# Attention and feed-forward on one core: softmax's two buffers alternate by batch, and side work of batches 3 to 7 is laid out over other steps

## The chip, the core and the metric

One core of a Trainium2 chip runs the whole program. TensorE (PE) multiplies matrices, VectorE (DVE) and ScalarE (ACT) work elementwise, GpSimd (POOL) hardly takes part, and SyncE (SP) issues the DMA transfers, all in one queue. Each engine works through its own instructions in order and waits at semaphores for the others. The metric is the device time of one execution in microseconds; lower is better.

## What is computed

```python
def attention(x, state):                 # B, H, S, D = 8, 8, 512, 64; state: 32 rows a head
    a = softmax(x @ state.T / sqrt(D));  xread = a @ state
    a2 = softmax(state @ x.T / sqrt(D)); sread = a2 @ x
    return concat([xread, sread])        # 544 rows for each of 8 batches, 512 columns

def ffn(x, w_in, w_out):                 # 4352 rows, 512 -> 2048 -> 512
    h = x @ w_in
    return (h - tanh(h)) @ w_out
```

All of it is float32. Matmuls run on operands that are split into a high and a low part (three products for one, lines 427 to 429 and 467 to 469); some small ones run on whole float32.

## The kernel before

**Chunks and steps.** The feed-forward part is the bulk. It runs in nine chunks: chunk `i` is batch `i`'s 512 rows of `xread` for `i` from 0 to 7, and chunk 8 is the 256 rows of `sread` of all batches. The 2048 hidden columns are taken in 16 pieces `f` of 128. One pair `(i, f)` is a step. `steps` lists them: 0 to 7 are the first half of chunk 0, 8 to 23 chunk 1, 24 to 31 the second half of chunk 0, and from 32 on chunks 2 to 8 with 16 steps each (batch 6 is steps 96 to 111). In a step `hidden` (six matmuls `hps`, lines 427 to 429) is written for the step two ahead (`LAG`), then `output` (twelve matmuls `ops`, lines 467 to 469) for the step itself. Between them `finish` makes `t = tanh(h)` on ACT, `t = h - t` on DVE (both line 435), and splits `t` into `g` (ACT line 119, DVE line 120). The bank that `hps` writes is one of two, so `hidden` of a step needs the subtraction of the step two before it.

**What attention leaves for it.** For chunk `i` the hidden piece is softmax times a product of state and input weights, `m`, which `load_m` brings in four loads a chunk (`mr`, line 241) and splits; for batches 6 and 7 a second addend `ml` is loaded and added on DVE (line 245). Softmax of batch `b` comes from `attention(b, aT)`, a generator whose pieces are: load `xT` and state (piece 0), scores `sps` on PE and softmax of each half (1 and 2), normalise, transpose and split into the tile `aT` for each half (3 and 4), then `state_read`.

**The state read.** `state_read` makes softmax over the other axis for each half (pieces 5 and 6). In each of them `regroup` transposes the half on DVE into `pe` (line 338), SP sends it to DRAM as `pd` (line 340) and loads it back in four transfers as `p2t` (line 343). Piece 7 is the read itself, 32 small matmuls `rps` (line 376), piece 8 scales it into `sr`. `pe` and softmax's tile `e` share two buffers. `xT` and `xn`, the input of the read, share two buffers too. Batches 0 and 1 do their softmax early and only their state reads late: `a0` and `late1` are such generators. At the end `turn_sread` regroups `sr` and splits it into `srT`, the input of chunk 8.

**Side work by a table.** The table `SCH` says at which step each piece of side work is written into the program: `att3` to `att7` hold the nine pieces of `attention` of batches 3 to 7, `a0` and `r1` the four of the late reads of batches 0 and 1, `m0` and `m1` the units that make `m`. `TURN` is the step of the first half of `turn_sread`. A step's side work may not be issued before that step's tanh and subtraction (`tc.issue_after`). Inside these bounds a scheduler sets the order on each engine from its own model, so that a piece can stand some steps away from its number.

**The two buffers.** `new_attention` takes one of two buffers for `aT`:

```python
aTs[b] = pool.tile([P, 2, 2, 512], F32R, tag="aT" if b % 4 in (1, 2) else "aT0", name=f"aT{b}", bufs=1)
```

So batches 3 and 4 follow each other in `aT0`, 5 and 6 in `aT`, batch 7 and then `srT` in `aT0`.

Of the kernel before, what the change touches and what calls it, by code (L numbers as in the profile page):

```python
# [9 lines left out]
F32R = mybir.dt.float32r  # L10
# [8 lines left out]
P = 128  # L19
# [12 lines left out]
LONE = 1  # L32
WHOLE_ROWS = 2
EARLY = 4
TURN = 123


@with_exitstack
def attention_ffn(ctx: ExitStack, tc: tile.TileContext, xT, xn, bd, bh, sp, sq, sm, sl, win, wout, xout, sout):
# [13 lines left out]
    pool = ctx.enter_context(tc.tile_pool(name="pool", bufs=2))  # L53
# [18 lines left out]
    wo = [cpool.tile([P, 2, DM], F32R, name=f"wo{f}") for f in range(NFF // 2)]  # L72
# [27 lines left out]
    pair = []  # L100
# [16 lines left out]
    def split(hi, lo, src, sub=None):  # L117

        nc.scalar.copy(hi, src)  # L119
        return (sub or nc.vector).tensor_sub(lo, src, hi)  # L120

    class Weight:
# [5 lines left out]
        def load(self):  # L128
            if self.src.dtype == F32:
                self.raw = next(raws)(f"{self.name}d", [P, 512], F32)  # L130
                dst = self.raw
            else:
                self.raw = next(raws)(f"{self.name}d", [P, 512, 2], U32)
                dst = self.raw.rearrange("p f w -> p (f w)")
            src = self.src.bitcast(dst.dtype)
            if len(src.shape) == 3:
                dst = dst.rearrange("p (r f) -> p r f", r=4)
            loadlog.append(nc.sync.dma_start(dst, src).ins)
# [19 lines left out]
                step()  # L158


    SCH = json.loads('{"conv": [8, 8, 9, 9, 11, 11, 12, 12], "pair": [10, 10, 13, 13], "a0": [57, 57, 59, 60], "att2": [12, 13, 13, 23, 27, 28, 29, 35, 39], "att3": [33, 38, 42, 43, 45, 46, 53, 55, 57], "att4": [54, 56, 60, 60, 60, 60, 60, 64, 67], "att5": [61, 69, 71, 71, 72, 72, 72, 74, 75], "att6": [87, 90, 90, 91, 93, 93, 94, 96, 98], "att7": [101, 101, 104, 104, 108, 108, 110, 112, 121], "m0": [19, 19, 19, 22, 22, 22, 22, 25, 25, 28, 28, 28, 30, 30, 30, 36], "m1": [50, 50, 53, 58, 61, 67, 67, 68, 77, 79, 79, 86], "wo": [8, 12, 12, 13, 13, 16, 19, 22], "r1": [75, 76, 79, 90], "at1": [8, 9], "at0": [10, 16], "plain": [1, 5, 6, 7]}')
    m_first = {}
    loadlog = []
    XH = int('5')
# [9 lines left out]
    def m_first_two(q, b):  # L174

        if b == 0:
            m = m_first[q] = pool.tile([P, 2, 512], F32, tag="mr", name=f"mr0{q}", bufs=RRB)
        else:
            m = m_second[q] = pool.tile([P, 2, 512], F32, tag=f"mr1{q}", name=f"mr1{q}", bufs=1)
        pss = [bank(ps_a, f"mps{b}{q}{k}") for k in range(2)]  # L180
        state_rows(pss, sps[:, 0, :, b], [wfs[q, r // 2][:, r % 2] for r in range(4)])
        for k in range(2):
            nc.scalar.copy(m[:, k], pss[k])
        if b == 0:
            nc.sync.dma_start(mdram[0][q][0].rearrange("g h n f -> (h n) g f"), m)
# [90 lines left out]
    def all_scores(b, bdr, xrs, pss=None):  # L276
        pss = pss or [bank(ps_a, f"sps{b}{hf}") for hf in range(2)]
        for j in reversed(range(4)):
            for hf in (0, 1) if b in SCH["plain"] else (1, 0):
                rs = slice(64 * hf, 64 * hf + 64)  # L280
# [53 lines left out]
    def regroup(src, name):  # L334


        e = pool.tile([P, 512], F32, tag="e", name=f"pe{name}")
        nc.vector.transpose(e, src)
        d = dram.tile([4, 32, 512], F32, name=f"pd{name}")
        nc.sync.dma_start(d.rearrange("j u x -> (j u) x"), e)  # L340
        dst = pool.tile([P, 4, 4, NS], F32, tag="p2t", name=f"p2t{name}", bufs=PTB)
        for c in range(4):
            nc.sync.dma_start(
                dst[32 * c : 32 * c + 32].rearrange("u j k n -> u j (k n)"),
                d[:, :, 128 * c : 128 * c + 128].rearrange("j u x -> u j x"),
            )
        return dst
# [42 lines left out]
    def turn_sread():  # L390
        turned = [regroup(sr[g].rearrange("p q k u -> p (q k u)"), f"t{g}") for g in range(2)]
        yield
        srT = pool.tile([P, 2, 4, 256], F32R, tag="aT0", name="srT", bufs=1)
        for g in range(2):
            hi, lo = (srT[:, i, :, P * g : P * g + P].rearrange("p k (b n) -> p k b n", b=4) for i in range(2))
            split(hi, lo, turned[g].rearrange("p b k n -> p k b n"))
        aTs[B] = srT
        yield
# [97 lines left out]
    aTs = [None] * (B + 1)  # L496
    ats = [[None] * 2 for _ in range(2)]

    def new_attention(b):
        aTs[b] = pool.tile([P, 2, 2, 512], F32R, tag="aT" if b % 4 in (1, 2) else "aT0", name=f"aT{b}", bufs=1)  # L500
        return attention(b, aTs[b])

    def advance(units, n=1):
        for _ in range(n):
            if next(units, 1) == 1:
                return
# [17 lines left out]
    def convert_win(q, p):  # L524
        if p % 2 == 0:
            wfs[q, p // 2] = pool.tile([P, 2, 512], F32, tag=("wf", "stage")[q - 2], name=f"w0{q}{p // 2}", bufs=WB)
        w0[q][p].convert(wfs[q, p // 2][:, p % 2])
        if p % 2:
            nc.sync.dma_start(wf[q][:, p - 1 : p + 1], wfs[q, p // 2])
# [317 lines left out]
    a0 = state_read(0, [ss[0], ss[1]])  # L847
# [3 lines left out]
    m1 = [m_units(g) for g in range(2)]  # L851
# [4 lines left out]
    wo_it = iter(range(HALF, NFF))  # L856

    turn = turn_sread()
    steps = [(0, f) for f in range(HALF)] + [(1, f) for f in range(NFF)] + [(0, f) for f in range(HALF, NFF)]
    steps += [(i, f) for i in range(2, B + 1) for f in range(NFF)]  # L860
    for st, (i, f) in list(enumerate(steps))[HALF:]:
        with ExitStack() as gates:
            for x in tanhs[st + (st < 2 * NFF)]:
                gates.enter_context(tc.issue_after(x))
            for _ in range(SCH["conv"].count(st)):
                convert_win(*next(convs))
                load(1)
            for _ in range(SCH["wo"].count(st)):
                x = next(wo_it)
# [12 lines left out]
        with ExitStack() as gates:  # L882
            for x in tanhs[st] if st < 2 * NFF else ():
                gates.enter_context(tc.issue_after(x))
            for _ in range(SCH["pair"].count(st)):
                m_first_two(*next(pairs))

        with ExitStack() as gates:
            if st < GATED:
                for x in tanhs[st]:  # L890
                    gates.enter_context(tc.issue_after(x))
            advance(a0, SCH["a0"].count(st))
            advance(second_split, SCH["at1"].count(st))
            advance(first_split, SCH["at0"].count(st))
            advance(late1, SCH["r1"].count(st))
            for b in range(2, B):
                n = SCH[f"att{b}"].count(st)
                if n:
                    if b not in atts:
                        atts[b] = new_attention(b)  # L900
                    advance(atts[b], n)
            for g in range(2):
                advance(m1[g], SCH[f"m{g}"].count(st))
            if st == TURN:
                advance(turn)
# [50 lines left out]
```

## Time and profile before

| what | value |
|---|---|
| median of 3 runs | 655.21 us (655.2 to 656.06) |
| the profiled execution | 655.09 us |
| its span, first to last instruction | 653.3 us |
| busy: PE, DVE, ACT | 640.9, 454.6, 347.1 us |
| granted TensorE clock, mean | 0.996 of full speed |
| DMA queue of SP | 104.56 MB, 49.9% of 16 engines |

The profile is of one execution. Busy time is the time in which an engine has an instruction in work; a matmul's printed duration overlaps with the next one, so that the pace of PE is read from the starts. "idle before" in brackets is how long the engine stood without work ahead of an instruction and whose event ended it.

### The profile page before, as it was taken

The page shows a single profiled execution, that of the slowest core. Times are in us where ns is not written, and L with a number is a line of the kernel's source. Part 1 is how long each engine was busy: PE and PEld are TensorE (multiplying, and loading weights), DVE is VectorE, ACT ScalarE, POOL GpSimd, SP SyncE. Part 2 cuts the span into 40 slices and gives each one's busy share as a digit, 9 for nine tenths or more (in the row PEclk, how much of TensorE's full clock was granted, in tenths as well). Part 3 has the DMA queues.
Part 4 walks back from the last instruction along what each step waited for, and adds up shares of the span by engine and source line. Part 5 has one row for each costly group of instructions (what it writes and reads, how often), then busy time and mean ns, then how long its engine had stood idle before and what let it go on. Part 6 is the DMA issues. An engine that isn't in the chain of part 4 may idle for free.

```text
span 653.3 us, 10246 instructions
## 1 busy us (share of the span) xinstructions
PE 640.9 (98%) x3818; PEld 504.6 (77%) x3818; DVE 454.6 (70%) x813; ACT 347.1 (53%) x629; POOL 0.7 (0%) x5
## 2 busy tenths in 40 slices
PE   8999999999999999999899999999799999999997
PEld 5456766888878788877677888887687888888996
DVE  5998999899584776566875985458756675464542
ACT  4864767777673545645455665444434443333442
POOL 0000000000000000000000000000000000000000
PEclk9999999999999999999999999999999999999999
DMA  8994786267786414446666248453542142021300
GB/s 317 379 312 149 255 282 262 55 194 221 241 281 188 131 57 137 130 137 193 198 204 174 92 153 277 129 161 133 173 150 97 33 129 97 1 77 53 130 32 33
DMA packets 65170, 105.34 MB, mean 161 GB/s; under 512 B 7648, under 2 KB 32224, under 8 KB 65120
## 3 DMA queue, kind: packets, MB, share of 16 engines
q1 hardware_dynamic: 64976, 104.56, 49.9%
q8 instruction: 30, 0.49, 0.3%
q14 instruction: 20, 0.16, 0.1%
q10 hardware_dynamic: 144, 0.13, 0.1%
HBM read 69.01 MB, written 35.65 MB: 160 GB/s over the span
## 4 chain that ended last, share of the span: by engine, by line
PE 86%; DVE 6%; DMA 5%; issue 1%; ACT 1%; SPq 0%; ACTq 0%; DVEq 0%
PE ops L467 17%; PE ops L469 17%; PE ops L468 17%; PE hps L427 9%; PE hps L429 8%; PE hps L428 8%; DMA pd<-pe 2%; PE hps L738 2%; PE mps L217 2%; PE rps L376 1%; PE mps L682 1%; PE ops L764 1%; PE mps L216 1%; DMA p2t<-pd 1%; DMA mearly<-e 1%
## 5 line engine op out<-in xcount | busy, mean ns | idle before, releaser
L467 PE MATMUL ops<-wo,g 128*128 128x512 f32 x536 | 213.7, 400 | 0.0
L468 PE MATMUL ops<-wo,g 128*128 128x512 f32 x536 | 209.0, 390 | 0.0
L469 PE MATMUL ops<-wo,g 128*128 128x512 f32 x536 | 196.2, 390 | 0.0
L435 DVE TENSOR_TENSOR t<-hps,t 128x512 f32<-128x512 f32 (+1 forms) x134 | 87.6, 655 | 90.1 <-ACT t L435 88.9
L435 ACT ACTIVATE t<-hps 128x512 f32<-128x512 f32 (+1 forms) x134 | 76.3, 572 | 135.4 <-PE hps L429 133.7
L467 PEld LDWEIGHTS ops<-wo,g 128*128 128x128 f32 x536 | 100.6, 188 | 26.1 <-issue 2.5
L469 PEld LDWEIGHTS ops<-wo,g 128*128 128x128 f32 x536 | 100.3, 188 | 24.2 <-issue 1.7
L468 PEld LDWEIGHTS ops<-wo,g 128*128 128x128 f32 x536 | 100.7, 188 | 22.1 <-issue 1.7
L119 ACT CAST g<-t 128x512 fp32r<-128x512 f32 (+1 forms) x134 | 79.5, 595 | 66.5 <-DVE t L435 59.6
L120 DVE TENSOR_TENSOR g<-t,g 128x512 fp32r<-128x512 f32 (+1 forms) x134 | 87.5, 655 | 31.1 <-ACT g L119 29.3
L427 PE MATMUL hps<-aT,m 128*128 128x512 f32 x232 | 91.2, 395 | 0.3 <-ACT aT L119 0.3
L428 PE MATMUL hps<-aT,m 128*128 128x512 f32 x232 | 90.9, 392 | 0.6 <-DVE aT L120 0.6
L429 PE MATMUL hps<-aT,m 128*128 128x512 f32 x232 | 90.3, 391 | 0.0
L427 PEld LDWEIGHTS hps<-aT,m 128*128 128x128 f32 x232 | 43.7, 189 | 12.9 <-DVE g L120 0.8
L428 PEld LDWEIGHTS hps<-aT,m 128*128 128x128 f32 x232 | 43.9, 189 | 10.7 <-DVE aT L120 1.0
L429 PEld LDWEIGHTS hps<-aT,m 128*128 128x128 f32 x232 | 43.7, 188 | 9.0
L120 DVE TENSOR_TENSOR m<-mr,m 128x1024 fp32r<-128x1024 f32 x29 | 35.4, 1219 | 10.7 <-ACT m L119 10.4
L120 DVE TENSOR_TENSOR wst<-w,wst 64x512 fp32r<-64x512 f32 (+1 forms) x56 | 36.3, 648 | 5.2 <-ACT wst L119 3.6
L119 ACT CAST m<-mr 128x1024 fp32r<-128x1024 f32 x29 | 30.3, 1043 | 7.7 <-DMA mr<-md 7.6
L119 ACT CAST wst<-w 64x512 fp32r<-64x512 f32 (+1 forms) x56 | 32.9, 587 | 0.7
L218 ACT COPY st<-mps 128x512 f32<-128x512 f32 (+1 forms) x56 | 30.1, 556 | 5.6 <-PE mps L217 4.2
L488 ACT COPY ob<-ops 128x512 f32<-128x512 f32 x19 | 11.1, 591 | 18.8 <-DMA out_x<-ob 14.4
(214 smaller groups left out, 609.0 us busy)
## 6 DMA issues: line engine op xcount, KB each, us to landing
md<-st SPq DMA_DIRECT2D x96, 128.0 KB, 2.3
mr<-md SPq DMA_DIRECT2D x20, 512.0 KB, 3.8
xT<-in_xT SPq DMA_DIRECT2D x16, 512.0 KB, 5.8
xn<-in_xn SPq DMA_DIRECT2D x16, 512.0 KB, 4.4
out_x<-ob SPq DMA_DIRECT2D x32, 256.0 KB, 3.0
w<-wf SPq DMA_DIRECT2D x12, 512.0 KB, 4.4
pd<-pe SPq DMA_DIRECT2D x16, 256.0 KB, 2.1
p2t<-pd SPq DMA_DIRECT2D x64, 64.0 KB, 2.6
```

The lines of the kernel that those rows point to most:

```text
L119: nc.scalar.copy(hi, src)
L120: return (sub or nc.vector).tensor_sub(lo, src, hi)
L217: nc.tensor.matmul(ps, s[:, 0, h], t[:, e], start=(g == 1), stop=True)
L218: nc.scalar.copy(stage[:, e], ps)
L427: nc.tensor.matmul(ps, mhi[k][:, cols], ahi[:, k], start=(k == 0), stop=False)
L428: nc.tensor.matmul(ps, mhi[k][:, cols], alo[:, k], start=False, stop=False)
L429: nc.tensor.matmul(ps, mlo[k][:, cols], ahi[:, k], start=False, stop=(k == nk - 1))
L435: tanhs.append((nc.scalar.activation(t, ps, AF.Tanh).ins, nc.vector.tensor_sub(t, ps, t).ins))
L467: nc.tensor.matmul(o, g[:, 0, tok], wo[f][:, 0], start=first, stop=False)
L468: nc.tensor.matmul(o, g[:, 0, tok], wo[f][:, 1], start=False, stop=False)
L469: return nc.tensor.matmul(o, g[:, 1, tok], wo[f][:, 0], start=False, stop=last).ins
L738: nc.tensor.matmul(hps[n], m[:, k], ats[b][k], start=(k == 0), stop=(k == 1))
```

## The change

The buffer of `aT` goes by odd and even batches, so that neighbours never share one; `srT` moves to the other buffer; the table's numbers for batches 3 to 7, the late reads and the units `m1` are others; `TURN` is three steps earlier. The table's line is cut to the entries that differ.

```diff
-TURN = 123
+TURN = 120
...
-"a0": [57, 57, 59, 60]
+"a0": [65, 66, 70, 71]
-"att3": [33, 38, 42, 43, 45, 46, 53, 55, 57]
+"att3": [36, 39, 40, 41, 43, 44, 45, 49, 51]
-"att4": [54, 56, 60, 60, 60, 60, 60, 64, 67]
+"att4": [49, 52, 53, 55, 57, 59, 60, 64, 65]
-"att5": [61, 69, 71, 71, 72, 72, 72, 74, 75]
+"att5": [70, 73, 74, 75, 76, 78, 79, 83, 84]
-"att6": [87, 90, 90, 91, 93, 93, 94, 96, 98]
+"att6": [83, 86, 87, 88, 90, 91, 92, 96, 97]
-"att7": [101, 101, 104, 104, 108, 108, 110, 112, 121]
+"att7": [102, 105, 106, 107, 108, 110, 111, 115, 117]
-"m1": [50, 50, 53, 58, 61, 67, 67, 68, 77, 79, 79, 86]
+"m1": [50, 51, 54, 58, 61, 62, 67, 68, 77, 80, 82, 85]
-"r1": [75, 76, 79, 90]
+"r1": [97, 98, 102, 103]
...
-        srT = pool.tile([P, 2, 4, 256], F32R, tag="aT0", name="srT", bufs=1)
+        srT = pool.tile([P, 2, 4, 256], F32R, tag="aT", name="srT", bufs=1)
...
-        aTs[b] = pool.tile([P, 2, 2, 512], F32R, tag="aT" if b % 4 in (1, 2) else "aT0", name=f"aT{b}", bufs=1)
+        aTs[b] = pool.tile([P, 2, 2, 512], F32R, tag="aT0" if b % 2 and b > 1 else "aT", name=f"aT{b}", bufs=1)
```

Three places show what the scheduler makes of it. In the names `t5_13` is `t` of chunk 5, piece 13, `pe61` the transpose of batch 6's second half, and the last number of a name only tells tiles apart.

The first place is DVE around batch 6's second transpose. Before:

```order
L435 TENSOR_TENSOR t5_15_4644<-hps5_15_4637,t5_15_4644 128x512
L120 TENSOR_TENSOR m61_4870<-mr61_4865,m61_4870 128x1024
L120 TENSOR_TENSOR aT6_4445<-at60_4596,aT6_4445 128x512
L361 TENSOR_SCALAR ri61_4715<-rs61_4713 128x1
L120 TENSOR_TENSOR g5_15_4647<-t5_15_4644,g5_15_4647 128x512
L338 STREAM_TRANSPOSE pe61_4720<-s61_4558 128x512
```

The same place now:

```order
L435 TENSOR_TENSOR t5_13_4522<-hps5_13_4515,t5_13_4522 128x512
L361 TENSOR_SCALAR ri61_4579<-rs61_4577 128x1
L338 STREAM_TRANSPOSE pe61_4584<-s61_4397 128x512
L362 RECIPROCAL ri61_4579<-ri61_4579 128x1
L120 TENSOR_TENSOR g5_13_4525<-t5_13_4522,g5_13_4525 128x512
```

The transpose stands behind the subtraction of piece 13 instead of piece 15, with one small row between instead of four; batch 6's read on PE stays where it was, ahead of the first output matmul of chunk 6.

The second place is PE at batch 4's scores (`sps40` and `sps41`, the two halves). Before:

```order
L281 MATMUL sps41_3022<-xT41_2936,bdr4_2932 32x512
L281 MATMUL sps40_3021<-xT41_2936,bdr4_2932 32x512
L281 MATMUL sps41_3022<-xT41_2936,bdr4_2932 32x512
L281 MATMUL sps40_3021<-xT41_2936,bdr4_2932 32x512
L281 MATMUL sps41_3022<-xT40_2934,bdr4_2932 32x512
L281 MATMUL sps40_3021<-xT40_2934,bdr4_2932 32x512
L281 MATMUL sps41_3022<-xT40_2934,bdr4_2932 32x512
L281 MATMUL sps40_3021<-xT40_2934,bdr4_2932 32x512
```

The same place now, with a step's matmuls left out between its two parts:

```order
L467 MATMUL ops3_0_2_2712<-wo4_76,g3_4_2806 128x512
L281 MATMUL sps41_2907<-xT41_2777,bdr4_2773 32x512 x2
L281 MATMUL sps41_2907<-xT40_2775,bdr4_2773 32x512 x2
L468 MATMUL ops3_0_2_2712<-wo4_76,g3_4_2806 128x512
...
L467 MATMUL ops3_0_2_2712<-wo5_77,g3_5_2854 128x512
L281 MATMUL sps40_2906<-xT41_2777,bdr4_2773 32x512 x2
L281 MATMUL sps40_2906<-xT40_2775,bdr4_2773 32x512 x2
L468 MATMUL ops3_0_2_2712<-wo5_77,g3_5_2854 128x512
```

The two halves alternated in one block; now four matmuls of one half stand a step ahead of the four of the other.

The third place is DVE at the end of chunk 6, where the third `mr` of chunk 7 is added (`mr72`, line 245). Before:

```order
L435 TENSOR_TENSOR t6_15_5250<-hps6_15_5243,t6_15_5250 128x512
L120 TENSOR_TENSOR m71_5447<-mr71_5442,m71_5447 128x1024
L120 TENSOR_TENSOR g6_15_5253<-t6_15_5250,g6_15_5253 128x512
L435 TENSOR_TENSOR t7_0_5280<-hps7_0_5273,t7_0_5280 128x512
L120 TENSOR_TENSOR g7_0_5283<-t7_0_5280,g7_0_5283 128x512
L245 TENSOR_TENSOR mr72_5550<-mr72_5550,ml72_5552 128x1024
L435 TENSOR_TENSOR t7_1_5325<-hps7_1_5318,t7_1_5325 128x512
```

The same place now:

```order
L435 TENSOR_TENSOR t6_15_5230<-hps6_15_5223,t6_15_5230 128x512
L355 TENSOR_REDUCE m271_5311<-s71_5135 128x1
L120 TENSOR_TENSOR aT7_4994<-at71_5207,aT7_4994 128x512
L357 TENSOR_SCALAR nm71_5313<-m271_5311 128x1
L120 TENSOR_TENSOR m71_5414<-mr71_5409,m71_5414 128x1024
L120 TENSOR_TENSOR g6_15_5233<-t6_15_5230,g6_15_5233 128x512
L361 TENSOR_SCALAR ri71_5317<-rs71_5315 128x1
L338 STREAM_TRANSPOSE pe71_5322<-s71_5135 128x512
L362 RECIPROCAL ri71_5317<-ri71_5317 128x1
L245 TENSOR_TENSOR mr72_5558<-mr72_5558,ml72_5560 128x1024
L435 TENSOR_TENSOR t7_0_5260<-hps7_0_5253,t7_0_5260 128x512
L435 TENSOR_TENSOR t7_1_5305<-hps7_1_5298,t7_1_5305 128x512
```

The add has moved ahead of the subtraction of chunk 7's first piece (`t7_0`), and batch 7's second transpose stands in the same stretch.

## Rows read from the trace of the kernel before

**Rows 1.** The page, part 1: busy time of TensorE.

```profile
PE 640.9 (98%) x3818; PEld 504.6 (77%) x3818; DVE 454.6 (70%) x813; ACT 347.1 (53%) x629; POOL 0.7 (0%) x5
```

**Rows 2.** What PE waited for: us in total, times, longest.

```profile
PE rps L376 <- DMA p2t<-pd: 5.4, 3, 3.3
```

**Rows 3.** Timeline of PE at batch 7's read: start us, us, instruction, [idle].

```profile
541.80 0.39 PE L429 MATMUL hps<-aT,m 128*128 128x512 f32 x1
542.12 1.10 PE L376 MATMUL rps<-xn,p2t 128*32 128x64 f32 x64
543.15 0.50 PE L467 MATMUL ops<-wo,g 128*128 128x512 f32 x1
...
544.18 0.39 PE L468 MATMUL ops<-wo,g 128*128 128x512 f32 x1
```

**Rows 4.** Timelines of PE and DVE: step 110's last hidden matmul, its subtraction.

```profile
525.48 0.39 PE L429 MATMUL hps<-aT,m 128*128 128x512 f32 x1
...
526.60 0.69 DVE L435 TENSOR_TENSOR t<-hps,t 128x512 f32<-128x512 f32 x1
```

**Rows 5.** Timeline of PE between 309 and 328 us.

```profile
309.56 0.39 PE L427 MATMUL hps<-aT,m 128*128 128x512 f32 x1
310.83 1.10 PE L376 MATMUL rps<-xn,p2t 128*32 128x64 f32 x64 [0.88 <-DMA p2t<-pd]
...
317.89 0.39 PE L468 MATMUL ops<-wo,g 128*128 128x512 f32 x1
...
324.09 1.09 PE L469 MATMUL ops<-wo,g 128*128 128x512 f32 x4
...
325.71 0.40 PE L429 MATMUL hps<-aT,m 128*128 128x512 f32 x1
327.25 1.10 PE L376 MATMUL rps<-xn,p2t 128*32 128x64 f32 x64 [1.14 <-DMA p2t<-pd]
```

**Rows 6.** Timeline of PE at batch 6's read; last row: busy time, granted clock.

```profile
467.24 0.40 PE L429 MATMUL hps<-aT,m 128*128 128x512 f32 x1
470.96 1.87 PE L376 MATMUL rps<-xn,p2t 128*32 128x64 f32 x62 [3.33 <-DMA p2t<-pd]
472.76 0.80 PE L427 MATMUL hps<-aT,m 128*128 128x512 f32 x1
...
474.58 0.40 PE L428 MATMUL hps<-aT,m 128*128 128x512 f32 x1
...
475.37 0.51 PE L427 MATMUL hps<-aT,m 128*128 128x512 f32 x1
...
470.90:474.40 3.50, 3.44 (x66) 3.00 (x67) 1.29 (x2) 1.10 (x2) 0.00 (x0) 0.53 0.47 129
```

**Rows 7.** Timeline of DVE: three transposes; DVE's busy time in a stretch.

```profile
300.69 0.71 DVE L338 STREAM_TRANSPOSE pe<-s 128x512 f32<-128x512 f32 x1 [2.19 <-DMA pd<-pe]
...
320.39 0.69 DVE L338 STREAM_TRANSPOSE pe<-s 128x512 f32<-128x512 f32 x1
...
461.82 0.71 DVE L338 STREAM_TRANSPOSE pe<-s 128x512 f32<-128x512 f32 x1
...
300.70:324.20 23.50, 20.36 (x45) 1.00 0.56 167
```

**Rows 8.** Timeline of PE: scores of batch 6, and of batch 0.

```profile
443.16 1.09 PE L281 MATMUL sps<-xT,bdr 64*32 64x512 f32 x16
...
9.58 1.08 PE L598 MATMUL sps<-xT,bdr 128*64 128x512 f32 x4
```

**Rows 9.** DMA issues: count, KB each, us to landing; `p2t` issues: ns min/median/max.

```profile
mr<-md SPq DMA_DIRECT2D x20, 512.0 KB, 3.8
xT<-in_xT SPq DMA_DIRECT2D x16, 512.0 KB, 5.8
...
pd<-pe SPq DMA_DIRECT2D x16, 256.0 KB, 2.1
...
L343 SPq DMA_DIRECT2D p2t<-pd x64: 302/426/1359, 165.7 to 533.1; - x64
```

More of the change, by code (lines that the diff above doesn't have):

```diff
@@ L158, in convert @@
                 step()
-    SCH = json.loads('{"conv": [8, 8, 9, 9, 11, 11, 12, 12], "pair": [10, 10, 13, 13], "a0": [57, 57, 59, 60], "att2": [12, 13, 13, 23, 27, 28, 29, 35, 39], "att3": [33, 38, 42, 43, 45, 46, 53, 55, 57], "att4": [54, 56, 60, 60, 60, 60, 60, 64, 67], "att5": [61, 69, 71, 71, 72, 72, 72, 74, 75], "att6": [87, 90, 90, 91, 93, 93, 94, 96, 98], "att7": [101, 101, 104, 104, 108, 108, 110, 112, 121], "m0": [19, 19, 19, 22, 22, 22, 22, 25, 25, 28, 28, 28, 30, 30, 30, 36], "m1": [50, 50, 53, 58, 61, 67, 67, 68, 77, 79, 79, 86], "wo": [8, 12, 12, 13, 13, 16, 19, 22], "r1": [75, 76, 79, 90], "at1": [8, 9], "at0": [10, 16], "plain": [1, 5, 6, 7]}')
+    SCH = json.loads('{"conv": [8, 8, 9, 9, 11, 11, 12, 12], "pair": [10, 10, 13, 13], "a0": [65, 66, 70, 71], "att2": [12, 13, 13, 23, 27, 28, 29, 35, 39], "att3": [36, 39, 40, 41, 43, 44, 45, 49, 51], "att4": [49, 52, 53, 55, 57, 59, 60, 64, 65], "att5": [70, 73, 74, 75, 76, 78, 79, 83, 84], "att6": [83, 86, 87, 88, 90, 91, 92, 96, 97], "att7": [102, 105, 106, 107, 108, 110, 111, 115, 117], "m0": [19, 19, 19, 22, 22, 22, 22, 25, 25, 28, 28, 28, 30, 30, 30, 36], "m1": [50, 51, 54, 58, 61, 62, 67, 68, 77, 80, 82, 85], "wo": [8, 12, 12, 13, 13, 16, 19, 22], "r1": [97, 98, 102, 103], "at1": [8, 9], "at0": [10, 16], "plain": [1, 5, 6, 7]}')
     m_first = {}
```

## The prediction

> **What bounds the kernel now.** I read the page first: TensorE (PE) is busy for 640.9 of 653.3 us [rows 1]. Work that moves off PE is therefore worth nothing unless PE waited for it, and the only stock to gain from is PE's 12 us without work, plus stretches in which it ran slowly. Next I read what PE waits for: the largest entry is the state read's matmuls (`rps`), which wait three times, 5.4 us in all, for the DMA that brings `p2t` [rows 2]. Then the timeline of PE around those three places, taken from the start of one matmul to the start of the next, since a restart costs more than the idle time printed. In an undisturbed stretch 72 matmuls take 16.32 us, 0.227 us each: from the row at 525.48 to the one at 541.80 [rows 3, 4]. An undisturbed state read starts 0.32 us after the matmul before it, lasts 1.03 us, and the four matmuls behind it take 1.03 us [rows 3].
>
> Against that scale the trace shows four losses. **(a)** Batch 0's late read: 309.56 to 310.83 is 1.27 us where 0.32 is normal: 0.95. **(b)** 317.89 to 324.09: 6.20 us for 18 matmuls (4.09): 2.11; the hidden matmuls of batch 4's first steps stand there. **(c)** Batch 4's read: 325.71 to 327.25, 1.54 for 0.32: 1.22 [rows 5]. **(d)** Batch 6's read: 467.24 to 470.96, 3.72 for 0.32: 3.40. Behind (d) PE has a granted clock of 0.53 for 3.5 us, nearly all at the lower of its two levels, 1.2 GHz: the read takes 1.80 instead of 1.03 and the next four matmuls 1.82 instead of 1.03, together 1.56 [rows 6]. One matmul of that read stands alone behind the rest: from 474.58 to 475.37, 0.79 us, lie it and two plain matmuls (0.45), so cutting it off cost 0.34 [rows 6]. Sum: 0.95 + 2.11 + 1.22 + 3.40 + 1.56 + 0.34 = 9.6 us.
>
> **Why those waits stand there.** A state read is a chain: DVE transposes into `pe`, SP sends it to DRAM (`pd`), SP loads it back in four pieces (`p2t`), PE reads it. From the end of the second transpose to the start of the read the chain took 6.2 us for batch 4 (321.08 to 327.25), 8.4 for batch 6 (462.53 to 470.96) and 9.4 for batch 0 (301.40 to 310.83) [rows 5 to 7]. One step of the loop is 18 matmuls, 4.1 us. The table of before puts batch 6's second transpose in the step two ahead of its read, DVE comes to it late, and 5.1 of the 8.4 us are covered. At (a) to (c) the reads of batches 0 and 4 and the softmax of batch 4 fall into the same steps: DVE is busy for 20.36 of 23.50 us, the transpose at 300.69 itself waits 2.19 us for a `pd` transfer, which still holds its buffer [rows 7], and batch 4's split into `aT0` must wait for batch 3's last hidden matmul, which reads that same buffer.
>
> **The change, part by part.** *The buffers.* Batches 3 and 4, and 5 and 6, no longer follow each other in one buffer. A split of batch b now needs batch b-2 to be finished, 16 steps earlier. This adds no instruction; `srT` gets batch 6's buffer, whose last reader is step 111, and is written from step 121 on. It takes away the ordering behind (b).
>
> *The table.* In the new order each read's second transpose stands earlier. The time it has, its cover, is the matmuls that PE's order puts between the hidden matmuls of the transpose's step and the read, times 0.227, less 0.9 us (DVE's subtraction starts 0.9 us after the step's last hidden matmul has passed: 525.48 + 0.227 to 526.60 [rows 4]), less DVE's rows before and with the transpose. For batch 6: 90 matmuls, 20.4 - 0.9 - 1.3 = 18.2 us. By the same count: batch 3 16, batch 4 22, batch 0 21, batch 5 21, batch 1 20. Against chains of 6.2 to 9.4 none of these waits, so (a), (c) and (d) go, and with (d) the slow clock and the lone matmul. Batch 7 is the exception. Its read stands at step 115 in the table, but the built order has its first four matmuls 64 matmuls behind step 111's hidden ones: 14.5 us, less 0.9, less DVE's rows (subtraction, maximum and the split of `aT` at 0.6 each, the 1024-wide split of `m` at 1.1, `g` 0.6, small ones 0.2, the transpose 0.6: 4.3): 9.3 us. The nearest chain is batch 6's, in which SP also issued an `mr` load ahead of the second `pd`: 8.4. I take no wait, with 0.9 to spare, and keep the other end, 9.4 and more, for a rival.
>
> *What it costs.* Batch 4's scores are no longer one block of eight matmuls but two of four, a step apart. The whole block lasts 1.09 us for its 16 records; the nearest row for fewer, scores of batch 0 in four records, lasts 1.08 [rows 8]. So a half costs between half a block (nothing more in sum) and a whole one (1.0 more, start to start); I take 1.0, by the four-record row. "TensorEngine Tiling (Array Packing)" of the Trainium skill, Key Properties, states that tiles operate independently and can run matmuls in parallel: a rule against this change, since a half then lasts as long as both; by it the sum would be the same 647.9, and no run here has shown a half block yet. Batch 3's read is cut into four runs of matmuls and batch 7's into two: four new cuts. Each costs between nothing and batch 6's 0.34; I take 0.34: 1.4.
>
> *DVE and ACT.* The same instructions are spread more evenly. By their durations the fullest five steps of the new order, 75 to 79, hold 21 us of DVE's rows in 20.4. A subtraction must be done before the hidden matmul two steps on, 30 matmuls or 6.8 us after its own, so DVE may lag by 4 to 5 us before PE stops. Nothing added here.
>
> *The wait it adds.* DVE's add of batch 7's third `mr` moved from behind `g` of step 112 to ahead of step 112's subtraction. It waits for the `mr` load, which SP issues behind the first half's `p2t`. That half's transpose ends 0.6 us after step 111's hidden matmuls by the count above; `pd` takes 2.1 to land and four issues 1.7, so the load starts at 4.4; 3.8 to land [rows 9] and 1.8 for add and subtraction end at 10.0, and PE needs that bank 48 matmuls, 10.9 us, behind step 111. Queued behind the add are the subtraction and, through it, `g`. Spare 0.9, so nothing; were that cover gone, each us that the load is late is a us of PE.
>
> **Sum.** The profiled execution took 655.09 us, 0.12 under the median shown, 1.8 of it outside the span. 655.09 - 9.6 + 1.0 + 1.4 = **647.9 us**. With both new costs at nothing 645.5.
>
> **Rivals.** *1. Batch 7 waits instead*, for its `p2t` or for the `mr` load. For it: 9.3 us of cover against batch 0's 9.4, and spares of 0.9 at both places. Against it: batch 4's 6.2, and this very read did not wait before [rows 3]. A wait of 1 to 2 us gives 649 to 650; one as long as batch 6's, with the slow clock, 3.4 + 1.6, gives 652.9. "TensorE: Matmul & The Clock Gate" of the Trainium skill, Part 1, puts the price of a throttled stretch at its length times the share of clock lost; on the 3.5 us here that is an estimate of 1.7, and the trace agrees with 1.56.
>
> *2. Only batch 6's loss goes.* (a) to (c), 4.3 us, come from DVE's backlog and move with it to steps 65 to 67 and 97 to 99, where a late read now meets the stores of a chunk. For it: DVE's 87% above. Against: the lag that the sums leave. 647.9 + 4.3 = 652.2.
>
> *3. The change doesn't do what it says*: rival 2, and batch 7 waits 2 to 3 us on top of it: 654.2 to 655.2.
>
> *4. Slower.* Batch 7's `xT` loads now wait for batch 1's read, which holds their buffers, 13.4 us of PE ahead of batch 7's scores. Less the read (1.0) and 5.8 to land [rows 9], 6.6 are spare. If SP stands held at an earlier wait, every us beyond that stops PE, and 1.6 of clock with it; 656.5 is reached at a hold of 13.6 us (6.6 + 8.6 - 1.6). For it: SP's queue is in order, and a load of step 99 and one of step 103 stand ahead. Against: what those two wait for is done before the read.
>
> **How the numbers follow.** Forecast 62 in 100 (own range 645.5 to 649), rival 1 23, rival 2 6, rival 3 4, rival 4 5. A measurement of this kernel can tell about 0.2%, 1.3 us, from no change, so faster means under 653.9: forecast and rivals 1 and 2, 0.90 with a little off; same 0.05, slower 0.05. The range runs from 645.8 (new costs near nothing) to 651.5, into rival 1 but not through it.
>
> **What would show it.** Right: no wait of `rps` for `p2t` among PE's waits, no stretch at the lower clock between 100 and 640 us, no idle PE between 305 and 330, batch 4's scores as two blocks of about 1 us each. Wrong, if `rps` or `hps` waits between 475 and 500, if the waits of (a) to (c) stand a chunk later, or if the score halves take 0.5 us each.

## The result, and the profile after

The changed kernel takes **648.27 us** (median of 4 runs, 648.01 to 649.14) against 655.3 us of the kernel before: a ratio of 0.9893, 95% interval 0.9875 to 0.991. The forecast was 647.9. The profiled execution took 648.01 us, its span is 646.2 us.

First the page of the changed kernel: busy time of the engines.

```profile
PE 639.8 (99%) x3818; PEld 503.4 (78%) x3818; DVE 453.7 (70%) x813; ACT 348.3 (54%) x629; POOL 0.7 (0%) x5
```

PE is busy 1.1 us less than in [rows 1] while the span is 7.1 us shorter: the gain is idle time that went, and some slow running: over the span the granted TensorE clock is 1.000 of full speed, 0.996 in the kernel before. What PE still waits for after its start-up is short (us in total, times, longest):

```profile
PE ops L467 <- ACT g L119: 0.3, 1, 0.3
PE hps L427 <- DVE t L435: 0.2, 1, 0.2
```

The row of [rows 2], 5.4 us of `rps` behind `p2t`, is gone. The first row stands at 180.7 us, ahead of everything that the change moves. The second, at 533.03, is the wait that the change adds. In two stretches (length; busy time of PE, PEld, DVE, ACT, POOL; granted clock, DMA share, GB/s):

```profile
100.00:640.00 540.00, 539.49 (x3003) 439.35 (x3001) 364.36 (x649) 282.94 (x504) 0.00 (x0) 1.00 0.45 141
300.70:324.20 23.50, 23.50 (x105) 19.48 (x104) 14.19 (x25) 13.84 (x26) 0.00 (x0) 1.00 0.60 179
```

Between 100 and 640 us PE lacks half a microsecond, the two rows above. The mean clock of so long a stretch would read 1.00 in the kernel before as well; in the changed kernel it is 1.00, the level of 2.4 GHz, in each single microsecond too. In the stretch of [rows 7] DVE is now busy for 14.19 us, not 20.36. Batch 4's and batch 6's reads stand as an undisturbed one does, 0.32 us behind the matmul before them:

```profile
325.18 0.39 PE L429 MATMUL hps<-aT,m 128*128 128x512 f32 x1
325.50 1.10 PE L376 MATMUL rps<-xn,p2t 128*32 128x64 f32 x64
...
464.74 0.39 PE L429 MATMUL hps<-aT,m 128*128 128x512 f32 x1
465.06 1.10 PE L376 MATMUL rps<-xn,p2t 128*32 128x64 f32 x64
```

The costs, from the same timeline: the first of the four runs of batch 3's read, and batch 4's two half blocks.

```profile
252.15 0.39 PE L429 MATMUL hps<-aT,m 128*128 128x512 f32 x1
252.47 0.41 PE L376 MATMUL rps<-xn,p2t 128*32 128x64 f32 x10
...
273.52 0.39 PE L467 MATMUL ops<-wo,g 128*128 128x512 f32 x1
273.84 1.06 PE L281 MATMUL sps<-xT,bdr 64*32 64x512 f32 x8
274.84 0.50 PE L468 MATMUL ops<-wo,g 128*128 128x512 f32 x1
...
279.16 1.06 PE L281 MATMUL sps<-xT,bdr 64*32 64x512 f32 x8
```

A half block lasts 1.06 us in 8 records, as long as a whole block in 16 [rows 8].

**A yardstick without the start.** Up to batch 2's read all engines' orders are the same in both kernels, yet that read starts at 197.87 us in the execution of before and at 197.37 in that of after:

```profile
197.37 1.10 PE L376 MATMUL rps<-xn,p2t 128*32 128x64 f32 x64
```

Over the twelve kernels of this study its start varies from 196.88 to 199.18 us. That is the execution's doing, not the kernel's. Below, **rest** is the span less this start: 653.3 - 197.87 = 455.4 us before, 646.2 - 197.37 = 448.8 after. The change is worth 6.6 us there. One profiled execution resolves much less than a microsecond of it: from this read to batch 7's scores the changed kernel takes 306.91 us (197.37 to 504.28), and e7 and e8 below, whose orders are the same up to there, take the same 306.91.

### The profile page after: what moved, and what is told of

Same layout as the page of the kernel before. It is cut to its first block, busy times and chain, and to the rows that moved or that the text cites. A ratio compares the mean times of both kernels' runs of the same rounds, so it can differ in the third digit from the quotient of the medians.

```text
span 646.2 us, 10241 instructions
## 1 busy us (share of the span) xinstructions
PE 639.8 (99%) x3818; PEld 503.4 (78%) x3818; DVE 453.7 (70%) x813; ACT 348.3 (54%) x629; POOL 0.7 (0%) x5
## 4 chain that ended last, share of the span: by engine, by line
PE 86%; DMA 5%; DVE 5%; SPq 1%; ACT 1%; issue 1%; ACTq 0%; DVEq 0%
PE ops L467 18%; PE ops L469 17%; PE ops L468 17%; PE hps L427 9%; PE hps L429 9%; PE hps L428 9%; DMA w05d<-in_win 2%; PE mps L217 2%; DMA mr<-md 1%; PE rps L376 1%; PE hps L738 1%; DMA sp<-in_sq 1%; PE sps L281 1%; PE mps L216 1%; PE mps L682 1%
## 5 line engine op out<-in xcount | busy, mean ns | idle before, releaser
L469 PE MATMUL ops<-wo,g 128*128 128x512 f32 x536 | 200.1, 390 | 0.0
L469 PEld LDWEIGHTS ops<-wo,g 128*128 128x128 f32 x536 | 100.2, 188 | 22.7 <-DVE t L435 0.8
L738 PE MATMUL hps<-at,mr 128*128 128x512 f32 x40 | 20.1, 600 | 0.1
```

Source lines behind the costliest of these rows:

```text
L469: return nc.tensor.matmul(o, g[:, 1, tok], wo[f][:, 0], start=False, stop=last).ins
L738: nc.tensor.matmul(hps[n], m[:, k], ats[b][k], start=(k == 0), stop=(k == 1))
```

## The experiments

Each ratio is to runs of the kernel before taken beside that run, whose medians are 655.3 to 656.4 us; the rest is from one execution.

| run | median, us | ratio to before, 95% | rest, us |
|---|---|---|---|
| the change | 648.27 | 0.9893, 0.9875 to 0.991 | 448.8 |
| e1, new buffers alone | 661.07 | 1.0084, 1.0063 to 1.0106 | 461.2 |
| e2, new table alone | 650.01 | 0.9917, 0.9896 to 0.9938 | 450.2 |
| e3, e1 and batch 6's numbers | 655.56 | 1.0001, 0.9988 to 1.0013 | 455.8 |
| e4, change with batch 6's old numbers | 654.07 | 0.9978, 0.9966 to 0.999 | 453.9 |
| e5, batches 3 and 4 whole | 645.45 | 0.9845, 0.982 to 0.9869 | 446.3 |
| e6, before with batch 0's read moved | 652.25 | 0.9936, 0.9919 to 0.9953 | 452.2 |
| e7, batch 7's read whole | 647.87 | 0.9881, 0.9859 to 0.9902 | 447.9 |
| e8, the add behind the subtraction | 648.33 | 0.9884, 0.9864 to 0.9904 | 448.5 |
| e9, e5 to e8's edits together | 645.64 | 0.9848, 0.9827 to 0.987 | 445.9 |
| e10, e5 and e7 together | 644.68 | 0.9821, 0.9801 to 0.9841 | 445.8 |

The theory was the prediction's: the table gives each read its cover, and the buffers take away an ordering behind loss (b). Rivals: the buffers do the work; the losses come from DVE's backlog and move with it; the change's own costs lie beside other work.

### e1: the buffers alone

```diff
 (kernel before)
-tag="aT" if b % 4 in (1, 2) else "aT0"
+tag="aT0" if b % 2 and b > 1 else "aT"
-srT = pool.tile([P, 2, 4, 256], F32R, tag="aT0", ...
+srT = pool.tile([P, 2, 4, 256], F32R, tag="aT", ...
```

> The kernel before with only the new buffer rule, its old table kept. The forecast's theory (the table gives each read its cover, the buffers only take away the ordering behind loss (b)): losses (a), (c) and (d) stay, the read of batch 6 still waits 3 to 3.6 us at a clock near half, and at most the 2.1 us of (b) go, so 653.1 to 655.3 us. Rival, the buffers do the work alone: under 650. Rival, the buffers give nothing: 655.3 and (b) still there.

Slower by 0.84%, 5.7 us in rest: none of the three. Loss (b) is still there, with late rows of DVE as its releasers, and batch 4's read waits 4.01 us, not the 1.14 of [rows 5]. PE and then SP in this run:

```profile
318.66 0.47 PE L217 MATMUL mps<-wst,sms 128*128 128x512 f32 x1 [0.20 <-DVE sr L383]
...
320.01 0.50 PE L427 MATMUL hps<-aT,m 128*128 128x512 f32 x1 [0.65 <-DVE ri L361]
...
325.30 0.39 PE L429 MATMUL hps<-aT,m 128*128 128x512 f32 x1
329.70 1.10 PE L376 MATMUL rps<-xn,p2t 128*32 128x64 f32 x64 [4.01 <-DMA p2t<-pd]
```

```profile
321.18 0.38 SPq L241 DMA_DIRECT2D mr<-md  x1
321.86 0.34 SPq L340 DMA_DIRECT2D pd<-pe  x1
323.59 0.78 SPq L224 DMA_DIRECT2D md<-st  x2
325.90 1.73 SPq L343 DMA_DIRECT2D p2t<-pd  x4
```

With the new buffer rule the scheduler orders these steps otherwise: the 512 KB `mr` load is issued ahead of batch 4's second `pd`, not behind it, and `pd` takes 4.0 us to land; `p2t` is issued at 325.90. In the kernel before `pd` went first and landed in 2.0 us, and `p2t` was issued at 323.14. The order is not all of it: the second transpose, with a split of `m` ahead of it on DVE, ends at 321.83 here and at 321.09 before. Counted from batch 2's read, batch 4's read starts 2.7 us later than in the kernel before, batch 5's scores 4.2 us, with the lower clock behind the wait, and batch 7's scores 5.7 us, with a longer wait at batch 6 (3.63 us) and a longer slow stretch behind it.

### e2: the table alone

```diff
 (changed kernel)
-tag="aT0" if b % 2 and b > 1 else "aT"
+tag="aT" if b % 4 in (1, 2) else "aT0"
-srT = pool.tile([P, 2, 4, 256], F32R, tag="aT", ...
+srT = pool.tile([P, 2, 4, 256], F32R, tag="aT0", ...
```

> The changed kernel with the old buffer rule, the new table kept. Its order cuts the reads of batch 4 (two runs of matmuls) and batch 6 (three) as well, three more cuts at 0.38 us, 1.1 in sum. The forecast's theory: every read keeps its cover, so the five p2t waits stay away, and batch 4's split waits at most 2 us for batch 3's last hidden matmul: 649.4 to 651.5 us. Rival, the new buffers are what makes the table possible: 653 or more, with rps waits back in PE's list. Rival, the table alone does it all: 648.3.

As the theory has it: no `rps` wait, 650.01 us, and 1.4 more in rest than the change, about the three more cuts (1.1 expected). So the table takes the waits away by itself. With this table the buffers are worth these cuts and no more.

### e3 and e4: batch 6's numbers

```diff
 (kernel before with the new buffers: e3)
-"att6": [87, 90, 90, 91, 93, 93, 94, 96, 98]
+"att6": [83, 86, 87, 88, 90, 91, 92, 96, 97]
 (changed kernel: e4)
-"att6": [83, 86, 87, 88, 90, 91, 92, 96, 97]
+"att6": [87, 90, 90, 91, 93, 93, 94, 96, 98]
```

> The kernel before with the new buffer rule and the new numbers of batch 6 alone. Its order makes batch 6's read one run of matmuls and cuts batch 6's scores into two blocks of four, 1.1 us. The forecast's theory: loss (d), 3.4 + 1.56 + 0.34 = 5.3 us, goes against the run with the buffers alone, less 1.1 for the scores: 4.2 us below it, 649 to 651; the waits of (a) and (c) stay. Rival, DVE's backlog makes the loss and moves with it: less than 2 us below the run with the buffers alone.

> The changed kernel with the old numbers of batch 6 alone: its second transpose stands again behind the subtraction of step 109, two steps ahead of the read, and one matmul of the read again stands alone. The forecast's theory: the wait of about 3.4 us comes back, with the lower clock behind it (1.6) and the lone matmul (0.34): 648.3 + 5.3 = 653.6, 652.9 to 654.3 us. Rival, the backlog theory, by which the lighter neighbourhood alone shortens the chain: the wait is under 2 us and the clock stays, 650 or less.

Against e1, e3 is 5.4 us shorter in rest and 5.5 in the median; the forecast was 4.2. The time itself missed the 649 to 651 expected, since e1 had come out slower than expected. The direction is the theory's. The size is larger because batch 6's loss in e1 was larger than in the kernel before: from batch 5's scores to batch 7's e3 takes 133.32 us and e1 139.17, 5.85 more, and e3 has a half block of 1.2 in it, so that e1 lost 7.0 there and not 5.3. In e4 the loss comes back, 5.1 us in rest where 5.3 were expected. Batch 6's read, first in e3, then in e4, and e4's clock there:

```profile
474.17 0.39 PE L429 MATMUL hps<-aT,m 128*128 128x512 f32 x1
474.49 1.10 PE L376 MATMUL rps<-xn,p2t 128*32 128x64 f32 x64
```

```profile
465.32 0.39 PE L429 MATMUL hps<-aT,m 128*128 128x512 f32 x1
468.89 1.93 PE L376 MATMUL rps<-xn,p2t 128*32 128x64 f32 x62 [3.18 <-DMA p2t<-pd]
```

```profile
468.90:472.30 3.40, 3.40 (x67) 3.01 (x68) 1.35 (x3) 1.10 (x2) 0.00 (x0) 0.60 0.46 144
```

e4 has the changed kernel's lighter neighbourhood everywhere else and still waits. Batch 6's numbers set this wait. That it is the place of the second transpose among them is argued from the chain and not shown alone, since all nine numbers moved: in e4 the transpose ends at 460.46, and its chain of 8.4 us is as long as in the kernel before; in e3 it ends 17.1 us ahead of the read.

### e6: what makes (a) to (c)

```diff
 (kernel before)
-"a0": [57, 57, 59, 60]
+"a0": [65, 66, 70, 71]
```

> The kernel before with the new numbers of batch 0's late read alone (65, 66, 70, 71 for 57, 57, 59, 60); old buffers, everything else of the old table. It asks what makes losses (a) to (c), 4.3 us. Theory of the backlog: DVE is overfull between 300 and 324 us because batch 0's read and batch 4's softmax fall together, so all three losses go where they stood, about 651.5 us, or up to 1 us more if batch 0's read waits at its new place. Theory of the ordering, as the prediction had it: loss (b), 2.1 us, comes from the order in the shared buffer and stays, so 653.5 or more with idle PE still between 317 and 324 us.

Old buffers, batch 4 where it was, and (a), (b) and (c) are all gone. PE is busy for the whole of the stretch, with DVE at 18.04 us; batch 4's and batch 0's reads do not wait:

```profile
300.70:324.20 23.50, 23.50 (x164) 19.24 (x163) 18.04 (x38) 12.70 (x25) 0.00 (x0) 1.00 0.49 137
```

```profile
321.49 0.39 PE L429 MATMUL hps<-aT,m 128*128 128x512 f32 x1
321.81 1.10 PE L376 MATMUL rps<-xn,p2t 128*32 128x64 f32 x64
...
361.02 0.39 PE L467 MATMUL ops<-wo,g 128*128 128x512 f32 x1
361.34 1.10 PE L376 MATMUL rps<-xn,p2t 128*32 128x64 f32 x64
```

Counted from batch 2's read to the matmul ahead of batch 6's read, the run gains 4.3 us. In rest it gains 3.2, since batch 6's loss is about 1.1 us larger here (its wait is 3.57 us, and more matmuls behind it run slowly). The ordering theory falls: (a) to (c) go with batch 0's read, old buffers or not. That it is DVE's busy time is not shown by this. In the kernel before DVE also stood still in these steps, 2.19 us at 300.69 [rows 7] and 2.77 us at 307.32, for a `pd` transfer that still held one of the two buffers that `pe` and `e` share:

```profile
307.32 0.71 DVE L307 STREAM_TRANSPOSE e<-s 128x512 f32<-128x512 f32 x1 [2.77 <-DMA pd<-pe]
```

e1 has both stops (2.07 and 2.82 us), e6 neither. A third buffer for these tiles, which would tell the stops from the load, was not tried.

### e5: batches 3 and 4 whole

```diff
 (changed kernel)
-"att3": [36, 39, 40, 41, 43, 44, 45, 49, 51]
+"att3": [36, 39, 40, 41, 43, 44, 45, 48, 50]
```

> The changed kernel with the last two numbers of batch 3 one step earlier (48 and 50 for 49 and 51). Its order puts batch 3's read in one run of 32 matmuls and batch 4's scores in one block of eight. By the profile of the changed kernel the half blocks cost 1.14 us more than one block and the three cuts of the read 1.13: 648.3 - 2.3 = 646.0 us. By the prediction's figures, 1.0 and 1.02: 646.3. Rival, the cost of a half block lies beside other work: 647.2. Rival, a read in one run needs more cover than it has and waits for p2t: 648.3 or more.

645.45 us, 2.5 less in rest. From the matmul ahead of batch 3's read to the one ahead of batch 4's scores PE takes 20.07 us here (252.27 to 272.34) and 21.37 in the changed kernel (252.15 to 273.52), with the same matmuls between: the three cuts cost 1.30. From there to the matmul ahead of batch 4's read it is 50.45 (to 322.79) against 51.66 (to 325.18): the second half block cost 1.21. Both were on PE's path, and a read in one run found its data there:

```profile
252.27 0.39 PE L429 MATMUL hps<-aT,m 128*128 128x512 f32 x1
252.59 1.10 PE L376 MATMUL rps<-xn,p2t 128*32 128x64 f32 x64
...
272.66 1.09 PE L281 MATMUL sps<-xT,bdr 64*32 64x512 f32 x16
```

### e7, e8, e9 and e10: batch 7's end

```diff
 (changed kernel: e7; with e5's edit as well: e10)
-"att7": [102, 105, 106, 107, 108, 110, 111, 115, 117]
+"att7": [102, 105, 106, 107, 108, 110, 112, 116, 118]
 (changed kernel: e8; with e5's and e7's edits: e9)
-                nc.vector.tensor_add(r, r, r2)
+                with tc.issue_after(tanhs[112][1]) if (b, q) == (7, 2) else ExitStack():
+                    nc.vector.tensor_add(r, r, r2)
```

> The changed kernel with the last three numbers of batch 7 one step later (112, 116, 118 for 111, 115, 117). The read of batch 7 then is one run of 32 matmuls, which takes away one cut of 0.34, and the add of the third mr stands four rows ahead on DVE, still in front of the first subtraction of chunk 7 and behind the same load. If the load sets the wait, the 0.49 us stay and the time is 648.3 - 0.34 = 647.9; if DVE's rows set it, the wait goes as well and it is 647.5. Rival, the second half's p2t now comes late behind the wait: 649 or more.

> The changed kernel with one rule more: DVE's add of batch 7's third mr may not be issued ahead of the subtraction of chunk 7's first piece. The theory of the added wait (the add stands at the head of DVE waiting for the mr load, the subtraction behind it comes late, and PE stands 0.2 us and loses 0.49 in sum): the wait of hps for that subtraction goes, 0.4 to 0.5 us less on PE's path, 647.8 us, at the limit of what the comparison can show; the timeline decides. Batch 7's read then comes about 0.9 us earlier, two matmuls and the wait: if its cover was spare by less than that, rps waits up to 0.5 us for p2t and the time is 648.3. Rival, the subtraction is late for another reason (DVE's backlog): the hps wait stays.

> The three edits together: batch 3's read and batch 4's scores whole, the add behind the subtraction, batch 7's numbers one step later (its order leaves one cut in batch 7's read). If the costs add up as the timeline has them, 1.14 + 1.13 + 0.49 = 2.8 us go: 645.5 us. If the added wait is put elsewhere, 646.0. Rival, one of the edits makes a new wait: 647 or more.

> The changed kernel with batch 3's last two numbers one step earlier and batch 7's last three one step later, no other edit: reads of batches 3 and 7 in one run each, batch 4's scores in one block. If the costs add up as each run alone showed them (2.5 us by the timeline for batches 3 and 4; the cut and the hps wait for batch 7, 0.8), 648.3 - 3.3 = 645.0 us. Rival: moving batch 3's read shifts the engines so that the wait at batch 7's add comes back: 645.5.

First the wait in the changed kernel, on DVE, SP and PE:

```profile
526.50 0.71 DVE L338 STREAM_TRANSPOSE pe<-s 128x512 f32<-128x512 f32 x1
...
531.15 1.23 DVE L245 TENSOR_TENSOR mr<-mr,ml 128x1024 f32<-128x1024 f32 x1 [3.90 <-DMA mr<-md]
532.29 1.28 DVE L435 TENSOR_TENSOR t<-hps,t 128x512 f32<-128x512 f32 x2
```

```profile
526.80 0.38 SPq L241 DMA_DIRECT2D mr<-md  x1
527.28 0.41 SPq L340 DMA_DIRECT2D pd<-pe  x1
531.75 1.74 SPq L343 DMA_DIRECT2D p2t<-pd  x4
```

```profile
532.42 0.39 PE L469 MATMUL ops<-wo,g 128*128 128x512 f32 x1
533.03 0.50 PE L427 MATMUL hps<-aT,m 128*128 128x512 f32 x1 [0.22 <-DVE t L435]
533.37 0.39 PE L428 MATMUL hps<-aT,m 128*128 128x512 f32 x1
```

The load is issued at 526.80 and lands 4.3 us later, DVE stands 3.90 us, and PE loses 0.38 + 0.11 = 0.49 us (533.03 less 532.42, less 0.227; then 0.34 for 0.23). In e8 the subtraction stands ahead of the add, and PE's row there has no wait. Batch 7's read starts 0.32 us behind its predecessor, without idle time, 8.9 us after the end of its transpose (528.12). In rows of DVE, then of PE:

```profile
527.42 0.70 DVE L338 STREAM_TRANSPOSE pe<-s 128x512 f32<-128x512 f32 x1
...
531.21 0.69 DVE L435 TENSOR_TENSOR t<-hps,t 128x512 f32<-128x512 f32 x1 [3.04 <-ACT t L435]
531.81 1.22 DVE L246 TENSOR_TENSOR mr<-mr,ml 128x1024 f32<-128x1024 f32 x1
```

```profile
533.49 0.39 PE L469 MATMUL ops<-wo,g 128*128 128x512 f32 x1
533.72 0.39 PE L427 MATMUL hps<-aT,m 128*128 128x512 f32 x1
...
536.66 0.39 PE L429 MATMUL hps<-aT,m 128*128 128x512 f32 x1
536.98 0.42 PE L376 MATMUL rps<-xn,p2t 128*32 128x64 f32 x12
```

By time e8 cannot be told from the change. From batch 7's scores to the last matmul the change takes 137.98 us and e8 137.58, 0.40 less. e8 alone does not show that the order did it: its load also landed 0.5 us sooner, counted from batch 7's scores, and with that the subtraction, which comes 0.33 us late in the change, would have been in time with the add in front as well. What supports the order is that PE idles there in five of the six kernels that have the add in front (0.11 to 0.22 us), and in none that has it behind. In the sixth, e7, the wait goes though the add still stands in front: it is free at 529.76, its load having been issued at 525.88, 0.4 us sooner counted from batch 7's scores, and landed in 3.8 us.

```profile
529.76 1.23 DVE L245 TENSOR_TENSOR mr<-mr,ml 128x1024 f32<-128x1024 f32 x1 [4.31 <-DMA mr<-md]
```

The read's second `pd` is issued 0.5 us behind this load in the changed kernel, in e7 not until 535.35. That this makes the load's landing longer is not shown: with the same `pd` behind it the load lands in 3.9 us in e8, and without it in 4.1 in e10. e7 gains 0.9 in rest, 0.34 for the cut and about 0.5 for the wait. e9 and e10 end alike, 2.9 and 3.0 us below the change in rest (2.8 and 3.3 expected). In e10 PE lost 0.38 us at this place again: counted from batch 7's scores its load was issued 0.5 us later than e7's and landed in 4.1 us. e9, whose subtraction does not stand behind the add, lost nothing there but has one cut more. **e10 has the lowest median here, 644.68 us, a ratio of 0.9821.** All of its interval lies below the change's, and it cannot be told from e9 and e5.

## Why the prediction was right

**The losses (9.6 us): right in size.** The rest fell by 6.6, and the costs below sum to 3.3, so 9.9 went. e10 gives the same without that sum: it has no cut and no half block, loses 0.38 us at the add, and is 9.6 shorter than the kernel before, so 10.0 went. e4 and e3 tie (d), the largest, to batch 6's numbers; e6 ties (a) to (c), 4.3 us, to batch 0's read in these steps. The covers held: batch 6's second transpose ends at 447.02 and its read starts at 465.06, 18.0 us for the 18.2 worked out.

**The buffers: wrong in mechanism.** "It takes away the ordering behind (b)" fell. In e1 the ordering is away and (b) stays; in e6 the ordering stays and (b) goes; e2 has the new table with the old ordering and no loss. In the kernel before DVE comes to the split of `aT` at 318.94, with no stop over 0.3 us since 307.32: it was late with everything. The buffers alone cost 5.7 us by the scheduler's other order, which the prediction did not consider since it costed them with the table. The sum did not suffer, because (b) was counted as gone either way.

**The half blocks: 1.0 predicted, 1.21 measured** (e5). The Trainium skill's rule gave the same sum ("TensorEngine Tiling (Array Packing)", Key Properties: independent tiles run matmuls in parallel). The trace now agrees: 1.06 us with 8 records, 1.09 with 16.

**The cuts: 0.34 each predicted.** Batch 3's three cost 1.30 by e5, 0.43 each. Batch 7's one stands in the changed kernel here:

```profile
536.57 0.39 PE L468 MATMUL ops<-wo,g 128*128 128x512 f32 x1
536.89 0.32 PE L376 MATMUL rps<-xn,p2t 128*32 128x64 f32 x8
537.14 0.73 PE L469 MATMUL ops<-wo,g 128*128 128x512 f32 x2
```

The second L469 starts at 537.48. In the 0.91 us from 536.57 lie two plain matmuls (0.45) and an eighth of the read (0.13), which leaves 0.33 for the cut. Sum 1.6 for 1.4.

**The added wait: 0 predicted with 0.9 spare, 0.49 measured.** The chain was 1.3 us longer than worked out. The last hidden matmul of step 111 starts at 521.54 and has passed at 521.77. The transpose ended 1.1 us after that (522.90), not 0.6, since DVE was still at the rows of the step before, one close behind the other. The load was issued 5.0 us after it, not 4.4, which is that same half microsecond and a little, and landed in 4.3, not 3.8. The errors are small and of one sign, and a spare of 0.9 did not hold them. By removing the wait e8 gave back 0.40.

**Batch 7's read: right.** Cover 9.3 against a chain of 8.4 was the narrowest place. In the changed kernel the transpose ends at 527.21 and the read starts at 536.89, 9.7 with the added wait in it. Its last `p2t` lands at 535.09: a chain of 7.9, not 8.4, and 1.8 us to spare. e8 takes that wait away and moves the read two matmuls up, and 8.9 us still suffice; the last `p2t` lands 1.2 us ahead of the read.

**The sum.** 9.9 removed, 1.21 + 1.30 + 0.34 + 0.49 = 3.3 added, 6.6 net where 7.2 was forecast. More was lost before than the prediction counted, and the new order cost more than it counted. That the median came out 0.4 us off, and the profiled execution 0.1, is partly luck: 0.5 us of the span came from the start, before the orders differ.

**The rivals.** 1 happened in its small form (the `mr` load, half a microsecond). 2 was right that (a) to (c) come from what falls together in those steps and not from the ordering, and wrong that they would move along: steps 65 to 71 took batch 0's read without a wait, in e6 too. 3 needed both in full and fell with them. 4 did not show: PE has no row of scores that waits.

## What to carry to other kernels

Price a late wait as a chain with its cover, link by link, and distrust a spare of less than one link's error. A constraint that stands next to a stall is not its cause until the stall has been seen to go without it: here the stall went with a second read in the same five steps, and lifting the constraint alone made the kernel slower, through another order of work and transfers. After a rearrangement look for work that was one block and is now cut in pieces; here two numbers of the table gave back another 2.5 us.

## What the runs showed of the hardware

- A 256 KB `pd` issued 0.5 to 0.7 us behind a 512 KB `mr` load on the same queue landed after 4.0 us (e1) and 4.5 us (the change); the twelve kernels have twelve such issues, at 3.95 to 4.95 us. Issued 1.1 us ahead of the load (before), or with no load beside it (e7), it took 2.0 and 2.2, and 2.0 to 2.9 in all issues that stand 0.4 to 1.9 us ahead of one. The order of two issues on SP is worth about 2 us of a chain.
- After a stop the lower clock did not always set in at the same place. Behind the 3.2 us stop of e4 the read itself ran slowly, 1.86 us to the next matmul. Behind the 4.0 us stop of e1 the read took its usual 1.04, and then matmuls came 0.41 to 0.43 us apart, the pace of the lower level, 1.2 GHz:

```profile
329.40:334.30 4.90, 4.59 (x73) 3.75 (x74) 1.45 (x3) 1.70 (x3) 0.00 (x0) 0.66 0.93 289
```

What tells the two apart was not tried.
- Executions of the same order of work differ by up to 2.3 us in the first 200 us, more than any of the new costs here. Counting from a row behind the start took that out: three kernels with the same order over the next 306.91 us agree there to 0.01 us.
